# Gated linear attention feeding an ELU feed-forward: one conversion of all weight pairs put on ScalarE, and a new hand-written order for the first ten spans

## The chip, the cores and the metric

The kernel runs on one core of one Trainium2 chip. The metric is the device time of one execution in microseconds (us), the median of several runs. The engines go by the profile's names: PE (matrix products; PEld is its weight load), DVE (VectorE), ACT (ScalarE), POOL (GpSimd) and SP (SyncE, which here issues the DMAs).

## The reference

Four batches of eight heads run a recurrence over 768 steps with a 48x48 state; the result goes, all heads side by side, through a feed-forward layer with an ELU. All inputs are fp32.

```python
for t in range(S):                                   # S = 768, D = 48
    state = alpha[:, :, t, :, None] * state + np.einsum('bhd,bhe->bhde', k[:, :, t], v[:, :, t])
    y[:, :, t] = np.einsum('bhd,bhde->bhe', q[:, :, t], state)
x = y.transpose(0, 2, 1, 3).reshape(B * S, H * D)    # 3072 x 384
h = x @ w_in                                         # 384 x 2048
g = np.where(h > 0, h, np.exp(np.minimum(h, 0)) - 1)
out = g @ w_out                                      # 2048 x 384
```

## The kernel before, in words

**The attention half** works on 24 windows of 128 steps (six per batch), all eight heads at once. For window i the tokens are: `L` (or `LA` and `LB`, its alpha part and its k and q part) loads k, q and alpha, `LV` loads v; `SC` (L214, DVE) scans alpha into running products P; `LN` and `EX` (L223, L228, ACT) make 1/P; `KA`, `KB`, `KC` (L236, L241 on DVE or POOL, L246 on DVE) scale k in three steps; `PC` (L250, ACT) copies P; `SQ` (L263 or L266) scales q; `TP` (L280, PE) transposes k and `KN` (L302, ACT) copies the transpose out of PSUM; `S` (L337 or L321) multiplies k with q, `MK` (L354 or L349, DVE) masks it; `U` (L384 or L366, PE) makes the state's update, `UP`, `UA`, `UB`, `UC` carry the state on; `YL` and `Y` (L445, L492 or L450, PE) give the window's output, with `Y3` (L479, ACT) between them in the first four windows. `XH` (L507, ACT) rounds the output to the upper half of a two-part number; `XL` (L531 on ACT or L533 on DVE) gives the rest; for windows 0 and 1 `XP` (L511, PE) first subtracts the upper part in PSUM.

**The feed-forward half** works on 12 blocks of 256 rows (two windows each) and eight slices j of the 2048 inner columns: `A.b.j` (L656, PE, 18 matmuls) makes h, `RA` and `RB` (L664, L669, ACT) and `RC` (L674, DVE) the ELU, `GH` (L680, ACT) and `GL` (L693, DVE) its two-part form, `O.b.j` (L707, PE, 12 matmuls) the product with w_out.

**The weights** are stored as fp64 and are made into two-part numbers on the chip. `F.f` (L560) loads one of 16 pieces of 768 KB; two pieces make a pair p (f = 0 and 2 are pair 0, f = 1 and 3 pair 1, f = 4 and 6 pair 2, f = 5 and 7 pair 3, and so on). `DA.p` (L577, DVE) shifts the lower words, `DB.p` turns the top byte of each number into the exponent bits by one multiply-add over 1536 bytes per partition, `DC.p` (L592, DVE) joins the two. Then `WH.f` (L620, ACT) rounds the upper part and `WL.f` makes the rest: on POOL or DVE (L640), but for f = 0 and 2 through PE (`WP`, L629 and L511) and ACT (L638). Before the change `DB` stands on DVE (L587) for pairs 0 and 1 and on ACT (L585) for the six others. `LC`, `CA` and `CB` only test the weights' range.

**The order** of everything is written out by hand. A string START lists 546 tokens (with `X.n`, n dummy matmuls on PE, L128), and the kernel issues them one after the other; then a template STEADY is laid out for each later pair of windows and block. Every engine works through its own instructions in the order of issue, so a token that waits holds back all later ones of that engine, and a DMA that waits on SP holds back the later DMAs. PSUM has eight buffers, the k, q and alpha tiles have three slots, the v tiles four. Twelve dummy matmuls stand ahead of START (`X(WARM)`), twelve more in it. START runs to the fifth slice of the fourth block; the rest of the kernel is STEADY.

Of the kernel before, what the change touches and what calls it, by code (L numbers as in the profile page):

```python
# [48 lines left out]


START = """
LA.0 X.2 SC.0 LN.0 LB.0 X.2 EX.0 SQ.0 LA.1 X.1 X.1 X.1 X.1 LV.0 X.1 LB.1 KA.0 SC.1 F.2 LN.1 KB.0 X.1 KC.0 X.1 EX.1 KA.1
PC.0 TP.0 KN.0 F.0 S.0 L.2 KB.1 SQ.1 MK.0 U.0 UA.0 KC.1 TP.1 YL.0 DA.0 S.1 UC.0 DB.0 LV.1 Y3.0 PC.1 L.3 KN.1 SC.2 LN.2
F.3 EX.2 DC.0 KA.2 SQ.2 Y.0 WH.0 U.1 MK.1 F.1 UP.1 UA.1 UC.1 WP.0 F.6 WH.2 YL.1 SC.3 F.4 XH.0 KB.2 LN.3 WP.2 KC.2 EX.3
Y3.1 SQ.3 XP.0 DA.1 WL.0 KA.3 PC.2 WL.2 LV.2 L.4 F.14 X.1 Y.1 DB.1 TP.2 XH.1 LV.3 S.2 KN.2 XP.1 KB.3 F.8 DA.2 XL.0 UB.0
KC.3 XL.1 DC.1 U.2 TP.3 DB.2 WH.1 A.0.0 F.5 UB.2 MK.2 RA.0.0 S.3 WL.1 UC.2 KN.3 UA.2 F.7 YL.2 RB.0.0 DC.2 U.3 F.10
A.0.1 WH.4 SC.4 WL.4 L.5 RC.0.0 LN.4 UA.3 SQ.4 WH.3 A.0.2 Y3.2 GH.0.0 MK.3 DA.3 YL.3 UB.3 EX.4 GL.0.0 WH.6 WL.6 Y.2
KA.4 WL.3 RA.0.1 RB.0.1 Y3.3 RC.0.1 Y.3 UC.3 RA.0.2 DB.3 RB.0.2 RC.0.2 A.0.3 KB.4 UB.1 XH.2 XH.3 GH.0.2 O.0.0 XL.2 XL.3
LV.4 DC.3 F.9 GH.0.1 RA.0.3 GL.0.1 A.1.1 A.1.2 GL.0.2 PC.3 DA.4 RB.0.3 RA.1.1 RC.0.3 GH.0.3 F.12 KC.4 TP.4 LV.7 RB.1.1
DB.4 RA.1.2 O.0.1 WH.7 RC.1.1 RB.1.2 DC.4 SC.5 A.1.0 WH.5 KN.4 L.6 F.11 GL.0.3 WL.5 LC.0 GH.1.1 RC.1.2 U.4 S.4 WH.8  # L60
PC.4 WH.10 DA.5 UB.4 UA.4 WL.7 O.0.2 GL.1.1 A.1.3 RA.1.0 WL.8 RB.1.0 GH.1.2 RC.1.0 RA.1.3 LV.5 L.7 O.0.3 GL.1.2 A.1.4
LN.5 EX.5 DA.6 GH.1.0 SQ.5 RA.1.4 DB.5 MK.4 RB.1.3 GL.1.0 UC.4 DB.6 KA.5 DC.5 RB.1.4 WH.11 WL.10 WH.9 DC.6 RC.1.3
RC.1.4 A.0.4 O.1.0 ZV.6 O.1.1 SC.6 GH.1.3 RA.0.4 RB.0.4 GL.1.3 GH.1.4 A.0.5 RC.0.4 LN.6 WL.11 O.1.2 WL.9 KB.5 WH.14
RA.0.5 GL.1.4 RB.0.5 WH.12 EX.6 RC.0.5 WL.14 O.1.3 O.1.4 GH.0.4 F.15 KC.5 LV.6 GH.0.5 GL.0.4 TP.5 S.5 KN.5 KA.6 PC.5
O.0.4 MK.5 KB.6 CA.0 SC.7 KC.6 WL.12 LN.7 A.0.6 U.5 F.13 GL.0.5 RA.0.6 DA.7 Y.4 UA.5 DB.7 EX.7 RB.0.6 PC.6 DC.7 A.0.7
XH.4 RA.0.7 XL.4 RB.0.7 A.1.7 RC.0.6 WH.13 KA.7 WH.15 WL.13 GH.0.6 O.0.5 RC.0.7 WL.15 GL.0.6 SQ.6 L.8 T.6 GH.0.7 RA.1.7
RB.1.7 GL.0.7 SQ.7 Y.5 A.1.5 XH.5 O.0.6 XL.5 RA.1.5 A.1.6 RC.1.7 GH.1.7 O.0.7 RB.1.5 RA.1.6 XD.4 RC.1.5 KB.7 TM.6 XD.5
RB.1.6 A.2.1 Z.0 RC.1.6 GH.1.5 CB.0 U.6 UA.6 GL.1.5 GH.1.6 KC.7 UB.6 UC.6 RA.2.1 LC.1 SC.8 O.1.5 PC.7 GL.1.6 A.2.0
GL.1.7 S.6 LN.8 RB.2.1 LV.8 S.7 SQ.8 MK.6 T.7 RA.2.0 EX.8 KA.8 O.1.6 RC.2.1 RB.2.0 A.2.3 GH.2.1 RC.2.0 GH.2.0 MK.7 KB.8
TM.7 O.1.7 A.2.2 KC.8 Z.1 GL.2.1 PC.8 GL.2.0 T.8 U.7 UA.7 S.8 MK.8 RA.2.3 CA.1 RA.2.2 Y.6 Y.7 UB.7 A.2.4 O.2.0 O.2.1  # L70
L.9 UC.7 SC.9 XH.6 RB.2.2 RB.2.3 LN.9 L.10 A.2.6 EX.9 RC.2.2 RC.2.3 XH.7 KA.9 GH.2.3 TM.8 LV.9 RA.2.4 XL.6 KB.9 RB.2.4
XL.7 GH.2.2 RC.2.4 SQ.9 CB.1 A.2.5 RA.2.6 KC.9 GH.2.4 GL.2.2 O.2.2 RA.2.5 PC.9 RB.2.6 S.9 GL.2.3 RB.2.5 GL.2.4 U.8 T.9
XD.6 UA.8 UB.8 RC.2.5 UC.8 GH.2.5 XD.7 SC.10 LC.2 TM.9 SQ.10 O.2.3 RC.2.6 A.2.7 LN.10 A.3.1 LV.10 RA.2.7 RB.2.7 GL.2.5
A.3.0 RA.3.1 RC.2.7 CA.2 O.2.4 CB.2 EX.10 MK.9 O.2.5 RB.3.1 LC.3 GH.2.6 GL.2.6 U.9 RA.3.0 O.2.6 RB.3.0 KA.10 RC.3.0
GH.3.0 RC.3.1 A.3.2 UA.9 LV.11 KB.10 UB.9 A.3.3 KC.10 L.12 L.11 UC.9 PC.10 T.10 GH.2.7 RA.3.2 GL.3.0 A.3.4 SC.11 GH.3.1
RB.3.2 GL.2.7 O.3.0 RA.3.4 LN.11 RC.3.2 EX.11 KA.11 GL.3.1 CA.3 SQ.11 O.3.1 RA.3.3 GH.3.2 CB.3 RB.3.3 RB.3.4 GL.3.2
KB.11 TM.10 RC.3.3 RC.3.4 GH.3.3 LC.4 GL.3.3 O.2.7 KC.11 PC.11 T.11 GH.3.4 Z.2 TM.11 O.3.2 GL.3.4
"""


# [10 lines left out]
def gla_elu_ffn(ctx: ExitStack, tc: tile.TileContext, qka, vv, vn, wgt, out):  # L91
    nc = tc.nc
# [487 lines left out]
    @tok  # L580
    def DB(p):

        word, top = parts(p)[1:]
        if p in (2, 3, 4, 5, 6, 7):
            nc.scalar.activation(out=word, in_=top, func=AF.Copy, scale=1.125, bias=-63.4375)  # L585
        else:
            nc.vector.tensor_scalar(out=word, in0=top, scalar1=1.125, scalar2=-63.4375, op0=ALU.mult, op1=ALU.add)  # L587
# [387 lines left out]
```

## Time and profile before

| | us |
|---|---|
| median of 3 runs | 496.06 |
| lowest and highest | 495.91 and 496.23 |
| the profiled execution: its own time | 494.32 |
| its span, first to last instruction | 492.6 |
| PE busy | 485.7 |
| ACT busy | 324.4 |
| DVE busy | 317.2 |
| POOL busy | 132.8 |

The busy time of an engine is the union of its instructions. For PE this says only that matmuls follow each other, since their ends are modelled. Where PE doesn't wait, the order of the other engines costs nothing; a wait of PE is time lost for good. The profiled execution was 1.7 us shorter than the median, and 1.7 us of its own time lie outside its span.

### The profile page before, as it was taken

The numbers are of one execution on the slowest core, as the hardware profiler recorded it, in microseconds if no ns is written. First come the engines' busy times: TensorE is split into PE (matmuls) and PEld (weight loads), VectorE is DVE, ScalarE is ACT, GpSimd is POOL, SyncE is SP. The second block draws the span as 40 slices with busy tenths as digits, with TensorE's granted clock in tenths as the row PEclk, the third lists the DMA queues.
The fourth block names the chain that finished last, engine by engine and source line by source line (L and its number), as shares of the span: only waits on it lengthen the run. The fifth ranks groups of instructions, "written<-read, shape, count | busy, mean of one in ns | idle before, by whom it ended". The sixth has DMA issues, their size and how long they took to land.

```text
span 492.6 us, 13059 instructions
## 1 busy us (share of the span) xinstructions
PE 485.7 (99%) x5348; PEld 469.4 (95%) x5348; DVE 317.2 (64%) x544; ACT 324.4 (66%) x759; POOL 132.8 (27%) x110
## 2 busy tenths in 40 slices
...
GB/s 316 413 415 312 190 2 206 27 110 99 177 53 207 40 150 164 110 104 153 142 81 177 134 78 187 95 110 193 81 126 130 73 133 41 33 38 13 1 35 37
DMA packets 42019, 63.89 MB, mean 130 GB/s; under 512 B 22496, under 2 KB 29408, under 8 KB 41952
## 3 DMA queue, kind: packets, MB, share of 16 engines
...
q8 instruction: 44, 0.72, 0.7%
q10 hardware_dynamic: 288, 0.39, 0.2%
...
HBM read 51.56 MB, written 4.72 MB: 114 GB/s over the span
## 4 chain that ended last, share of the span: by engine, by line
PE 98%; DVE 0%; issue 0%; ACT 0%; DVEq 0%
PE h L656 42%; PE o L707 41%; PE y L450 4%; PE q L321 2%; PE q L366 2%; PE y L445 2%; PE wp L128 2%; PE sc L337 1%; PE tp L280 1%; PE y L492 1%; PE wd L629 1%; PE u L384 0%; PE u L410 0%; PE wd L511 0%; DVE st L354 0%
## 5 line engine op out<-in xcount | busy, mean ns | idle before, releaser
L656 PE MATMUL h<-xt,w 128*128 128x256 f32 x1728 | 216.2, 281 | 0.1
L656 PEld LDWEIGHTS h<-xt,w 128*128 128x128 f32 x1728 | 210.4, 188 | 1.6 <-PE q L366 0.2
L707 PE MATMUL o<-w,gh 128*128 128x384 f32 x768 | 197.1, 338 | 0.0
L707 PEld LDWEIGHTS o<-w,gh 128*128 128x128 f32 x768 | 136.0, 188 | 0.4
L707 PE MATMUL o<-w,gl 128*128 128x384 f32 x384 | 129.3, 337 | 0.0
L674 DVE SCALAR_TENSOR_TENSOR h<-r,h 128x512 f32<-128x512 f32 x96 | 65.6, 692 | 89.2 <-ACT r L669 88.3
L664 ACT ACTIVATE r<-h 128x512 f32<-128x512 f32 x96 | 56.2, 593 | 56.7 <-PE h L656 53.8
L680 ACT CAST gh<-h 128x512 fp32r<-128x512 f32 x96 | 55.4, 583 | 45.4 <-DVE h L674 35.6
L266 POOL TENSOR_TENSOR st<-qka,P 64x512 f32<-64x512 f32 x38 | 46.1, 1214 | 112.4 <-issue 109.7
L707 PEld LDWEIGHTS o<-w,gl 128*128 128x128 f32 x384 | 72.2, 188 | 0.0
L693 DVE TENSOR_TENSOR gl<-h,gh 128x512 fp32r<-128x512 f32 x96 | 63.6, 678 | 10.5 <-ACT gh L680 9.5
L669 ACT ACTIVATE r<-r 128x512 f32<-128x512 f32 x96 | 60.4, 632 | 1.5
L236 POOL TENSOR_TENSOR qka<-qka,R 128x512 f32<-128x512 f32 x19 | 25.8, 1360 | 100.4 <-ACT R L228 85.2
L611 ACT ACTIVATE ck<-ck,lim 128x384 f32<-128x384 f32 x64 | 41.7, 652 | 1.7
L349 DVE TENSOR_TENSOR st<-q,mask 64x256 f32<-64x256 f32 x80 | 33.8, 422 | 6.3 <-PE q L321 2.4
L214 DVE TENSOR_TENSOR_SCAN P<-qka,first 128x516 f32<-128x516 f32 x24 | 35.4, 1474 | 2.1 <-DMA qka<-in_qka_dram 1.8
L241 POOL TENSOR_TENSOR R<-P,R 128x512 f32<-128x512 f32 x20 | 27.9, 1394 | 17.0 <-DVE qka L236 10.1
L223 ACT ACTIVATE R<-P 128x512 f32<-128x512 f32 x24 | 15.1, 627 | 16.0 <-DVE P L214 16.0
L287 DVE STREAM_TRANSPOSE R<-qka 128x512 f32<-128x512 f32 x18 | 19.9, 1105 | 8.8 <-ACT R L250 8.8
L403 DVE TENSOR_TENSOR vs<-vs,q 48x192 f32<-48x192 f32 (+1 forms) x36 | 12.6, 350 | 15.3 <-PE q L366 14.9
L250 ACT ACTIVATE R<-P 128x512 f32<-128x512 f32 x24 | 15.1, 629 | 10.4 <-DVE qka L246 10.4
L450 PE MATMUL y<-st,vs 128*64 128x64 f32 x640 | 21.1, 224 | 0.0
...
## 6 DMA issues: line engine op xcount, KB each, us to landing
...
```

The lines of the kernel that those rows point to most:

```text
L214: nc.vector.tensor_tensor_scan(out=P.rearrange("p n w -> p (n w)"), data0=t[:, 2 * NP * W:], data1=first.rearrange("p n w -> p (n w)"), in ...
L266: eng(SQV, i).tensor_tensor(out=st[r, a], in0=d["q"][r], in1=pw(i)[r], op=ALU.mult)
L349: nc.vector.tensor_tensor(out=d["st"][r, a, :, c * C:(c + 1) * C], in0=d["s4"][a][o], in1=mask[o].unsqueeze(1).broadcast_to([64, NP, C]), ...
L450: nc.tensor.matmul(out[64 * a:64 * a + m], lhsT=lhs(i, c, a)[:, n * D:n * D + m], rhs=d["st"][:, a, n, c * C:(c + 1) * C], start=start, st ...
L611: nc.scalar.activation(out=t[:, :, k], in_=t[:, :, 1], func=AF.Relu, scale=sign, bias=bias, accum_out=chk_w[:, k, f:f + 1])
L656: nc.tensor.matmul(h[:, f, :], lhsT=t[:, wi, ws], rhs=x[:, c, xi, :], start=(f == 0 and k == 0), stop=(k == 8), skip_group_check=True)
L664: nc.scalar.activation(out=r, in_=d["h"], func=AF.Relu, scale=-1.0)
L669: nc.scalar.activation(out=d["r"], in_=d["r"], func=AF.Exp, scale=-1.0)
L674: nc.vector.scalar_tensor_tensor(out=d["h"], in0=d["r"], scalar=-1.0, in1=d["h"], op0=ALU.add, op1=ALU.max)
L680: nc.scalar.copy(out=gh, in_=d["h"])
L693: nc.vector.tensor_tensor(out=gl, in0=d["h"], in1=d["gh"].bitcast(F32), op=ALU.subtract)
L707: nc.tensor.matmul(o[:, 0:DM], lhsT=gt[:, f, ms], rhs=t[:, wi, f * DM:f * DM + DM], start=(j == 0 and f == 0 and k == 0), stop=(j == NJ - ...
```

## The change

It does two things. `DB` goes to ACT for all eight pairs, so that the branch for DVE falls away. And START is written anew: the same 546 tokens, as a set, in another order. STEADY and all other code stay as they are; instructions behind `DB` have line numbers that are smaller by three (L656 is L653 in the changed kernel, L707 is L704).

```diff
 START = """
-LA.0 X.2 SC.0 LN.0 LB.0 X.2 EX.0 SQ.0 LA.1 X.1 X.1 X.1 X.1 LV.0 X.1 LB.1 KA.0 SC.1 F.2 LN.1 KB.0 X.1 KC.0 X.1 EX.1 KA.1
+X.2 LA.0 SC.0 LA.1 X.2 LB.0 LB.1 X.1 F.2 LV.0 X.1 F.0 LN.0 LV.1 X.1 SC.1 EX.0 KA.0 X.1 KB.0 KC.0 X.1 X.1 X.1 X.1 LN.1
...
     def DB(p):
 
         word, top = parts(p)[1:]
-        if p in (2, 3, 4, 5, 6, 7):
-            nc.scalar.activation(out=word, in_=top, func=AF.Copy, scale=1.125, bias=-63.4375)
-        else:
-            nc.vector.tensor_scalar(out=word, in0=top, scalar1=1.125, scalar2=-63.4375, op0=ALU.mult, op1=ALU.add)
+        nc.scalar.activation(out=word, in_=top, func=AF.Copy, scale=1.125, bias=-63.4375)
```

**DVE at the very start**, before the change. The scan L214 makes P of a window; `qka0` is the tile of window 0, `qka1` that of window 1, `st_136` the masked product of window 0.

```order
L214 SCALAR_TENSOR_TENSOR P_128<-qka0_120,first_89 128x516
L236 TENSOR_TENSOR qka0_120<-qka0_120,R_130 128x512
L214 SCALAR_TENSOR_TENSOR P_147<-qka1_121,first_89 128x516
L241 TENSOR_TENSOR R_130<-P_128,R_130 128x512
L246 SCALAR_TENSOR_TENSOR qka0_120<-R_130,qka0_120 128x512
L236 TENSOR_TENSOR qka1_121<-qka1_121,R_151 128x512
L263 TENSOR_TENSOR st_187<-qka1_121,P_147 128x512
L354 TENSOR_TENSOR st_136<-sc_168,mask_85 128x2x4x64
L246 SCALAR_TENSOR_TENSOR qka1_121<-R_151,qka1_121 128x512
L577 TENSOR_SCALAR wm_221<-raw0_149 128x1536
```

The same place in the changed kernel (`st_158` is the masked product of window 0):

```order
L214 SCALAR_TENSOR_TENSOR P_128<-qka0_120,first_89 128x516
L214 SCALAR_TENSOR_TENSOR P_145<-qka1_121,first_89 128x516
L236 TENSOR_TENSOR qka0_120<-qka0_120,R_141 128x512
L241 TENSOR_TENSOR R_141<-P_128,R_141 128x512
L246 SCALAR_TENSOR_TENSOR qka0_120<-R_141,qka0_120 128x512
L236 TENSOR_TENSOR qka1_121<-qka1_121,R_156 128x512
L246 SCALAR_TENSOR_TENSOR qka1_121<-R_156,qka1_121 128x512
L263 TENSOR_TENSOR st_205<-qka1_121,P_145 128x512
L354 TENSOR_TENSOR st_158<-sc_170,mask_85 128x2x4x64
L577 TENSOR_SCALAR wm_232<-raw0_136 128x1536
```

The scan of window 1 no longer stands between the three steps on window 0's k, and window 1's last step (L246) no longer waits behind the mask of window 0 (L354).

**SP, from the second load of window 1 on**, before the change (`raw0` and `raw1` are weight pairs 0 and 1, `qka2` is window 2; the second `qka0` is window 3, in the slot of window 0):

```order
L183 DMA qka1_121<-in_qka_dram 128x1024
L560 DMA raw0_149<-in_wgt_dram 128x6144 x2
L175 DMA qka2_122<-in_qka_dram 128x1540
L191 DMA vs1_106<-in_vv_dram 128x768
L175 DMA qka0_120<-in_qka_dram 128x1540
L560 DMA raw1_253<-in_wgt_dram 128x6144 x2
L560 DMA raw2_315<-in_wgt_dram 128x6144 x2
```

And in the changed kernel:

```order
L183 DMA qka1_121<-in_qka_dram 128x1024
L560 DMA raw0_136<-in_wgt_dram 128x6144
L191 DMA vs0_105<-in_vv_dram 128x768
L560 DMA raw0_136<-in_wgt_dram 128x6144
L191 DMA vs1_106<-in_vv_dram 128x768
L175 DMA qka2_122<-in_qka_dram 128x1540
L560 DMA raw1_244<-in_wgt_dram 128x6144 x2
L175 DMA qka0_120<-in_qka_dram 128x1540
L560 DMA raw2_277<-in_wgt_dram 128x6144
```

Window 3's tile (L175 into `qka0`) was the tenth DMA and is now the twelfth, behind both pieces of weight pair 1; the set of the first twelve is the same.

**ACT from window 3's logarithm to the rest of window 1's output**, before the change (L223 and L228 are `LN.3` and `EX.3`, L638 the casts of `WL.0` and `WL.2`, L507 `XH.1`, L302 `KN.2`, L531 `XL.0` and `XL.1`):

```order
L223 ACTIVATE R_333<-P_327 128x512
L228 ACTIVATE R_333,chk_p_114<-R_333 128x512
L479 COPY y3_343<-y_318 128x128
L638 CAST w0_284<-wd_309 128x384
L638 CAST w0_284<-wd_312 128x384
L250 ACTIVATE R_251,chk_p_114<-P_249 128x512
L638 CAST w0_284<-wd_335 128x384
L638 CAST w0_284<-wd_338 128x384
L507 ACTIVATE xt_330,chk_y_115<-y_318 128x3x128
L302 COPY kn_416<-tp_392 128x512
L531 CAST xt_330<-y_214 128x3x128
L531 CAST xt_330<-y_318 128x3x128
```

And in the changed kernel, where L584 is the multiply-add of pair 1 and L635 are the casts:

```order
L584 ACTIVATE raw1_244<-raw1_244 128x2x768
L223 ACTIVATE R_347<-P_345 128x512
L228 ACTIVATE R_347,chk_p_114<-R_347 128x512
L635 CAST w0_317<-wd_327 128x384
L635 CAST w0_317<-wd_330 128x384
L531 CAST xt_342<-y_237 128x3x128
L507 ACTIVATE xt_342,chk_y_115<-y_308 128x3x128
L302 COPY kn_413<-tp_389 128x512
L635 CAST w0_317<-wd_320 128x384
L635 CAST w0_317<-wd_323 128x384
L531 CAST xt_342<-y_308 128x3x128
```

The conversion of pair 1 now stands ahead of `LN.3`; two casts, `XL.0` and `XH.1` stand between `EX.3` and `KN.2`, and `PC.2` is behind this place.

On PE the twelfth dummy of START goes from behind `XP.0` to the dummies ahead of `TP.0`; `WP.2` and `WP.0` follow each other where `YL.1` stood between them; `S.3` and `TP.3` change places; `TP.4` goes from behind `A.1.2` to the place ahead of `Y.3`, and `U.4` to the place ahead of `O.0.0`. At the end of START, POOL has `SQ.10` behind `SQ.11` instead of far ahead of it.

More of the change, by code (lines that the diff above doesn't have):

```diff
@@ L51 @@
 START = """
-LA.0 X.2 SC.0 LN.0 LB.0 X.2 EX.0 SQ.0 LA.1 X.1 X.1 X.1 X.1 LV.0 X.1 LB.1 KA.0 SC.1 F.2 LN.1 KB.0 X.1 KC.0 X.1 EX.1 KA.1
[L53 to L76, printed above, removed]
@@ L77 @@
-KB.11 TM.10 RC.3.3 RC.3.4 GH.3.3 LC.4 GL.3.3 O.2.7 KC.11 PC.11 T.11 GH.3.4 Z.2 TM.11 O.3.2 GL.3.4
+X.2 LA.0 SC.0 LA.1 X.2 LB.0 LB.1 X.1 F.2 LV.0 X.1 F.0 LN.0 LV.1 X.1 SC.1 EX.0 KA.0 X.1 KB.0 KC.0 X.1 X.1 X.1 X.1 LN.1
+SQ.0 TP.0 EX.1 KN.0 KA.1 KB.1 S.0 KC.1 U.0 SQ.1 MK.0 UA.0 L.2 TP.1 S.1 DA.0 PC.0 KN.1 YL.0 F.3 F.1 PC.1 UC.0 Y3.0 MK.1
+U.1 DB.0 SC.2 LN.2 UP.1 L.3 F.4 LV.2 DC.0 UA.1 Y.0 EX.2 KA.2 YL.1 WH.2 WH.0 WP.2 F.6 WP.0 UC.1 DA.1 F.5 Y3.1 KB.2 F.7
+XH.0 DB.1 SC.3 LN.3 EX.3 SQ.2 KC.2 SQ.3 KA.3 XP.0 Y.1 WL.0 TP.2 XL.0 XH.1 S.2 KN.2 LC.0 KB.3 XP.1 KC.3 DA.2 U.2 LV.3
```

22 lines of the change are left out of this document (added).

## The prediction

> **What bounds the kernel now.** I read the page first, then the waits of PE, then PE's, DVE's and ACT's timelines of the first 45 us. The page's rows of busy time and of the chain that ended last:
>
> ```profile
> PE 485.7 (99%) x5348; PEld 469.4 (95%) x5348; DVE 317.2 (64%) x544; ACT 324.4 (66%) x759; POOL 132.8 (27%) x110
> PE 98%; DVE 0%; issue 0%; ACT 0%; DVEq 0%
> ```
>
> PE is the chain for 98% of the span. The stretches of the span (length, then busy time of PE, PEld, DVE, ACT and POOL, the granted clock, the DMA share, GB/s) say where it isn't busy:
>
> ```profile
> 0.00:5.00 5.00, 2.92 (x7) 1.04 (x8) 2.81 (x10) 1.28 (x1) 2.83 (x13) 1.00 0.60 202
> 5.00:10.00 5.00, 4.60 (x20) 1.96 (x19) 3.40 (x5) 2.99 (x7) 1.19 (x1) 1.00 1.00 381
> 10.00:15.00 5.00, 4.74 (x118) 4.09 (x117) 4.51 (x8) 2.17 (x8) 1.56 (x1) 1.00 1.01 420
> 15.00:20.00 5.00, 5.00 (x89) 4.27 (x89) 4.94 (x7) 3.58 (x8) 1.57 (x1) 1.00 1.02 415
> 20.00:25.00 5.00, 5.00 (x62) 3.42 (x62) 4.91 (x7) 4.26 (x13) 0.00 (x0) 1.00 1.02 412
> 25.00:30.00 5.00, 5.00 (x115) 4.44 (x110) 4.18 (x6) 3.56 (x7) 0.00 (x0) 1.00 1.02 414
> 30.00:35.00 5.00, 4.87 (x102) 4.55 (x102) 5.00 (x5) 3.07 (x6) 3.34 (x1) 1.00 1.02 414
> ```
>
> PE has lost time until 15 us and 0.13 us at 33 us, and nothing else before the tail. DVE is full from 15 to 25 and from 30 to 35 us, the DMA engines from 5 to 35 us. PE's own waits, all of them:
>
> ```profile
> PE wp L128 <- DVE first L122: 2.1, 1, 2.1
> PE tp L280 <- issue: 0.4, 1, 0.4
> PE tp L280 <- DVE qka L246: 0.3, 1, 0.3
> ```
>
> So the same 546 tokens in another order can win about a microsecond here, and lose any amount.
>
> **The change part by part.** PE's timeline at the places that move (start, busy time, the group, the idle time before it):
>
> ```profile
> 2.08 7.22 PE L128 MATMUL wp<-first 128*128 128x512 bf16 x23 [2.08 <-DVE first L122]
> 9.71 0.63 PE L280 MATMUL tp<-ident,qka 128*128 128x128 f32 x4 [0.40 <-issue]
> ...
> 12.88 0.66 PE L280 MATMUL tp<-ident,qka 128*128 128x128 f32 x4 [0.26 <-DVE qka L246]
> ...
> 23.20 0.39 PE L128 MATMUL wp<-first 128*128 128x512 bf16 x1
> 23.52 0.88 PE L492 MATMUL y<-y,sel 128*64 128x128 f32 x12
> ...
> 27.89 0.68 PE L366 MATMUL q<-vs,kn 64*64 64x48 f32 x32
> ...
> 42.04 1.60 PE L445 MATMUL y<-st,vs 48*48 48x64 f32 x48
> ...
> 45.78 0.52 PE L707 MATMUL o<-w,gh 128*128 128x384 f32 x2
> ```
>
> and DVE's:
>
> ```profile
> 6.43 0.73 DVE L236 TENSOR_TENSOR qka<-qka,R 128x512 f32<-128x512 f32 x1 [1.45 <-ACT R L228]
> 7.08 1.22 DVE L214 TENSOR_TENSOR_SCAN P<-qka,first 128x516 f32<-128x516 f32 x1
> 8.22 0.66 DVE L241 TENSOR_TENSOR R<-P,R 128x512 f32<-128x512 f32 x1
> 8.91 0.69 DVE L246 SCALAR_TENSOR_TENSOR qka<-R,qka 128x512 f32<-128x512 f32 x1
> ...
> 26.20 0.96 DVE L577 TENSOR_SCALAR spare<-raw 128x1536 int32<-128x1536 int32 x1 [0.82 <-DMA raw<-in_wgt_dram]
> ```
>
> *TP.0.* It waits for `KC.0`, which ended at 9.60. The scan of window 1 (1.22) goes ahead of `KA.0`, into the 1.45 in which DVE waits for ACT, so `KA.0` at 6.43, `KB.0` and `KC.0` follow each other (0.73, 0.66, 0.69) and end about 8.5 us. But PE is in order and now has 24 dummies ahead of `TP.0` instead of 23: 7.22 us end at 9.30, and one more costs at most 0.27 (16 of them in the 4.3 us from 5 to 9.3). `TP.0` starts at about 9.55: -0.15. Bounds: 0, should `KA.0` be held back by a POOL product until 7.2, and -0.4, all the idle time there.
>
> *TP.1.* Its 0.26 of waiting goes if `KC.1` ends before `U.0` does, which is 2.9 us behind the start of `TP.0` (12.88 - 0.26 - 9.71), at 12.45. `EX.1` follows `EX.0` on ACT and ends near 7.7; `KA.1` starts behind `KC.0` at 8.5 (0.7), `KB.1` on POOL took up to 1.57 (row below), `KC.1` 0.69: about 11.5, a cover of 0.9, if nothing holds them up. -0.26; bounds 0 and -0.4, with the restart.
>
> *The dummy at 23.20* holds PE for 0.32 until `Y.1` starts. At the start it lies in the waiting for `TP.0`, already counted. -0.32; at worst -0.15, if the change of kind in the array costs the rest.
>
> *The 0.13 at 33 us* lies in `U.3`, which now comes behind two `A` groups: -0.13; bounds 0 and -0.3, should the restart behind it have cost as much again.
>
> *The conversions.* The two forms of it and the steps behind it (busy time, mean ns of one, idle time before), then rows of the timelines of ACT and POOL:
>
> ```profile
> L585 ACT ACTIVATE raw<-raw 128x1536 int32<-128x1536 uint8 x6 | 9.8, 1632 | 0.0
> L587 DVE TENSOR_SCALAR raw<-raw 128x1536 int32<-128x1536 uint8 x2 | 1.9, 954 | 0.0
> L592 DVE SCALAR_TENSOR_TENSOR wm<-raw,wm 128x1536 int32<-128x1536 int32 x4 | 7.2, 1796 | 0.7 <-ACT raw L585 0.7
> L620 ACT CAST w<-wm 128x768 fp32r<-128x768 f32 x8 | 6.5, 826 | 0.2 <-DVE wm L592 0.2
> ```
>
> ```profile
> 21.11 0.63 ACT L223 ACTIVATE R<-P 128x512 f32<-128x512 f32 x1 [0.49 <-DVE P L214]
> 21.77 0.63 ACT L228 ACTIVATE R<-R 128x512 f32<-128x512 f32 x1
> 22.31 0.18 ACT L228 ACTIVATION_READ_ACCUMULATOR R<-R 128x1 f32 x1
> ...
> 22.55 0.86 ACT L638 CAST w<-wd 128x384 fp32r<-128x384 f32 x2
> ...
> 25.96 0.49 ACT L507 ACTIVATE xt<-y 128x384 fp32r<-128x384 f32 x1 [1.17 <-PE y L445]
> 26.54 0.59 ACT L302 COPY kn<-tp 128x512 f32<-128x512 f32 x1
> ```
>
> ```profile
> 18.30 1.57 POOL L241 TENSOR_TENSOR R<-P,R 128x512 f32<-128x512 f32 x1 [6.22 <-DVE qka L236]
> 30.83 3.34 POOL L640 TENSOR_TENSOR w<-spare,w 128x768 fp32r<-128x768 f32 x1 [10.96 <-ACT w L620]
> ```
>
> DVE is rid of 2 x 0.95 = 1.9 us, ACT gets 2 x 1.63 = 3.3. From 15 to 35 us ACT was busy for 3.58 + 4.26 + 3.56 + 3.07 = 14.5 of 20 us; it will be for 17.7. That fits, so the conversions as such cost nothing; what they may cost is the lateness of the ACT steps behind them, each of which PE needs. [...]
>
> *The new order around it.* The place where the cover is thinnest: window 3's load was the tenth transfer and is the twelfth. Before, the fourteenth (`F.4`) landed when `DA.2` could start, at about 26.1; two pieces of 768 KB lie between, at 412 GB/s 1.9 us each, so the twelfth lands near 22.3. Then, one behind the other: `SC.3` 1.22, `LN.3` 0.66, `EX.3` with its read 0.72, the two casts of `WL.0` 0.8, `XL.0` 0.49 (as `XH`, the same size), `XH.1` 0.58, `KN.2` 0.59. That is 5.1 us, so `KN.2` ends at 27.4. `U.2` needs it. PE gets to `U.2` at 27.89 - 0.15 - 0.26 - 0.32 = 27.15. A wait of 0.2 is new; bounds 0 and +0.6 (the landing may be some tenths off, since it is worked out from a rate).
>
> *Covered.* Pair 0's conversion follows `Y3.0` on ACT, at about 14.8, and ends at 16.5; `DC.0` 1.80 and two casts of 0.83 make 20.0, and PE asks for the second one at about 20.1, behind `U.1`, `UP.1`, `Y.0`, `YL.1` and the first piece of `WP`. If it is late, PE waits as long; I take nothing. `TP.4` comes earlier, ahead of `Y.3`: PE had 17.9 us from `U.2` to the first `O` (27.89 to 45.78), about 2.4 of them `Y.3` (0.88 and 1.60); so it is at `TP.4` at 27.35 + 15.5 = 42.8. `KC.4` stands on DVE behind `SC.4`, which follows window 3's masks at about 35, `DC.3` 1.80 and five steps of about 0.69 (`KC.0`'s), it is the sixth: 35 + 1.2 + 1.8 + 4.1 = 42.1, a cover of 0.7. Weight pair 3 lands earlier, ahead of its use. STEADY and the tail have the same instructions, and PE waits for nothing there; `SQ.10`, which STEADY reads, is one POOL pair (2.5 us) later than `SQ.11` was, ahead of a first product some 9 us behind it:
>
> ```profile
> 199.85 2.48 POOL L266 TENSOR_TENSOR st<-qka,P 64x512 f32<-64x512 f32 x2
> ```
>
> ```profile
> 211.32 0.66 PE L321 MATMUL q<-st,qka 48*64 48x64 f32 x32
> ```
>
> The sum on the profiled execution: 494.32 - 0.15 - 0.26 - 0.32 - 0.13 + 0.2 = 493.66, that is -0.66, say -0.7. The median of the runs is 1.74 above the profiled one; the same difference taken from it gives 495.4.
>
> **The rivals.** *All covers hold, all gaps close* (faster): TP.0 -0.4, TP.1 -0.4, the dummy -0.32, `U.3` -0.3, nothing new: -1.4, 494.6. Speaks for it that these gaps are all that PE has lost; against it that the dummies themselves fill the first.
>
> *ACT's queue becomes the bound from 20 to 35 us* (slower). It is in order, and `WL`, `XL`, `XH`, `KN` stand behind two conversions and behind window 3's logarithm. PE is held one for one at `U.2` or at `A.0.1` from the point at which `KN.2` ends after 27.15; one conversion on that path is +1.63, so -0.86 + 0.2 + 1.63 = +1.0, 497.0; both are 498.7. A landing of window 3 at 24 us or later does the same. For it: 17.7 of 20 us, and the 0.2 is already the wrong way. Against it: from 10 to 20 us ACT had 4.2 us free, and pair 1's conversion ends (22.0) before window 3 lands (22.3). [...]
>
> *A POOL product holds DVE up ahead of `TP.4`* (no change). This row stood beside the POOL row of 30.83 above:
>
> ```profile
> 32.40 2.86 DVE L214 TENSOR_TENSOR_SCAN P<-qka,first 128x516 f32<-128x516 f32 x1
> ```
>
> The scan took 2.86 instead of 1.23 while POOL's product ran. In the new order `SC.4` stands beside the first such product of pair 2 (about 33 to 36 us), with `DC.3`, `WL.4` and `KC.4` behind it: 1.6 late, of which the cover takes 0.7, so 0.9 is given back: -0.7 + 0.9 = +0.2, 496.3. [...]
>
> *The gaps close, but PE meets the next late input and waits there instead* (no change): 496.1.
>
> **How the numbers follow.** My forecast has 0.40, from 495.0 to 496.0; all gaps close 0.25; ACT the bound 0.18; POOL ahead of `TP.4` 0.12; nothing won 0.05. A measurement of this kernel tells about 0.2%, 1.0 us, from no change (the runs before lie within 0.32 us). Faster by more than that are the second case and a small part of the first (0.06): 0.31. Slower is the third: 0.18. The rest, 0.51, is the same. The range reaches from the second case's 494.6 to one exposed conversion, 497.0; what lies beyond are 0.05 below and about 0.1 above.
>
> **What would show it.** Right: `TP.0` at 9.5 to 9.6 without idle time, `TP.1` right behind `U.0`, no dummy behind `XP.0`, PE at its first `O` group no later than before less 0.7 (without `TP.4` and `U.4`), PE full from 13 us on but for some tenths at `U.2`. Wrong: PE idle in front of L366 or L653 between 25 and 45 us with ACT as the releaser, or in front of `TP.4` with DVE; window 3's scan after 24 us; any gap of PE behind 50 us; or a faster kernel by over 1.0 us with no wait gone that is named here.

## The result, and the profile after

The changed kernel took 498.03 us (median of 20 executions, 495.57 to 502.99); the kernel before, beside it, 496.09 (20 executions, 493.92 to 496.74). The ratio is 1.0063, with a 95% interval of 1.0042 to 1.0084: slower by 0.63%. The forecast was 495.4 with a range to 497.0.

The 20 executions are not one crowd. Five stand at 500.43 to 502.99 with a mean granted clock of 0.983 to 0.988, on average 502.27; the other fifteen average 497.52 with 0.996 to 1.00; before averaged 495.78. So 1.19 of the 2.93 us between the two means (498.71 and 495.78) are the five. The profiled execution is one of them: 502.74 us, span 501.0, clock 0.983. Its page, the row of busy time and the chain by engine:

```profile
PE 491.1 (98%) x5348; PEld 474.2 (95%) x5348; DVE 318.3 (64%) x542; ACT 326.9 (65%) x761; POOL 133.9 (27%) x110
PE 97%; DMA 1%; issue 0%; POOL 0%; SPq 0%; ACT 0%; POOLq 0%
```

PE is busy for 5.4 us more with the same 5348 products, and a DMA, SP and POOL have come onto the chain, where before had only DVE and ACT beside PE. The stretches that the prediction showed of before (length, busy time of PE, PEld, DVE, ACT, POOL, granted clock, DMA share, GB/s):

```profile
5.00:10.00 5.00, 4.24 (x18) 1.67 (x16) 3.14 (x3) 2.59 (x6) 1.68 (x1) 1.00 0.96 349
10.00:15.00 5.00, 3.99 (x70) 3.61 (x71) 3.67 (x7) 0.71 (x2) 1.18 (x1) 0.76 1.04 429
15.00:20.00 5.00, 5.00 (x76) 4.46 (x76) 2.66 (x4) 3.58 (x8) 0.00 (x0) 0.50 1.01 412
20.00:25.00 5.00, 5.00 (x56) 4.14 (x53) 3.72 (x4) 3.11 (x7) 1.18 (x1) 0.50 1.02 417
25.00:30.00 5.00, 5.00 (x41) 3.64 (x37) 3.73 (x5) 3.49 (x8) 0.00 (x0) 0.87 1.01 408
```

From 15 to 30 us PE reads as full; the granted clock, third from the end of the row, is the column that tells. (The clock's record begins only when the clock first comes up: until then, about 5.8 us here, the column reads 1.00 although the dummies start 0.427 us apart instead of 0.216.) Two things stand here: PE lost 1.8 us around 10 us, and then ran at half clock. The beginning of the chain of the first 35 us gives the first:

```profile
1.74 6.06 DMA qka<-in_qka_dram
...
7.95 1.69 POOL st L263
9.64 1.37 issue
11.01 0.63 PE tp L280 x4
```

The DMA is `LB.0`, issued third instead of second, as the new order has `LA.1` ahead of it: it lands at 7.80. The chain goes on with POOL's `SQ.0`, which waits for that landing and in before started at 5.42; the step that ends right ahead of `TP.0` is `KC.0`, at 10.90 in DVE's rows. DVE's rows of the changed kernel go on from there:

```profile
3.72 2.36 DVE L214 TENSOR_TENSOR_SCAN P<-qka,first 128x516 f32<-128x516 f32 x2 [0.83 <-DMA qka<-in_qka_dram]
7.90 0.69 DVE L236 TENSOR_TENSOR qka<-qka,R 128x512 f32<-128x512 f32 x1 [1.82 <-DMA qka<-in_qka_dram]
8.63 1.55 DVE L241 TENSOR_TENSOR R<-P,R 128x512 f32<-128x512 f32 x1
10.21 0.69 DVE L246 SCALAR_TENSOR_TENSOR qka<-R,qka 128x512 f32<-128x512 f32 x1
```

and POOL's, the step beside them:

```profile
7.95 1.68 POOL L263 TENSOR_TENSOR st<-qka,P 128x512 f32<-128x512 f32 x1 [4.32 <-DMA qka<-in_qka_dram]
```

They say that `KA.0` starts 1.47 later than before (7.90, was 6.43). `KB.0` stands beside `SQ.0` and takes 1.55 instead of 0.66, which uses up 0.89 of what the scan's new place wins. `TP.0` starts at 11.01 instead of 9.71: +1.30. The two scans do lie ahead, as forecast.

The second, in half microseconds:

```profile
12.50:13.00 0.50, 0.50 (x15) 0.43 (x12) 0.20 (x1) 0.00 (x0) 0.26 (x1) 0.60 0.99 406
...
26.00:26.50 0.50, 0.50 (x11) 0.43 (x8) 0.50 (x1) 0.02 (x1) 0.00 (x0) 0.75 0.95 393
```

A mean of 0.60 in 12.5 to 13.0 is a fall from 1.00 to 0.50 at 12.6, one of 0.75 a return at 26.25: 13.65 us at half. It doesn't double a group's time:

```profile
12.64 2.12 PE L384 MATMUL u<-vs,kn 128*64 128x48 f32 x32
14.69 1.11 PE L280 MATMUL tp<-ident,qka 128*128 128x128 f32 x4
15.73 1.97 PE L337 MATMUL sc<-st,qka 48*64 48x64 f32 x32
```

The same groups take 1.27, 0.66 and 1.15 at full clock (rows under e1): 1.7 times. So 13.65 us at half lose about 13.65 x (1 - 1/1.7) = 5.6. PE's last products, from the chain of before and of after:

```profile
485.91 2.79 PE o L707 x16
```

and

```profile
485.92 9.12 PE o L704 x52
```

The two chains' products end at 488.70 and 495.04: +6.34, of which 1.30 and 5.6 make 6.9; the rest, about 0.6, is won between. The other 2.1 us of the two spans (492.6 and 501.0) lie behind PE's last product: 3.9 us there before, 6.0 here. Most of it is the transfer of the last output, 1.84 us there and 3.92 here. This is not the change's doing: of the four profiled executions of the changed kernel two have 6.0 and 6.4 us there and two 3.9, and the times of before lie in two groups, near 494.3 and near 496.4, with little between. So a median of twelve can swing by a microsecond, and single steps are judged below by PE's rows. The ratios below leave out an execution that is more than 1.5% longer than the fastest of its kernel, which takes one away from each of e1 (527.79 us, with a clock of 0.85), e6, e7, e12 and e13; but for e1's, these are executions with the half clock, and the medians and the counts of half clocks have them.

### The profile page after: what moved, and what is told of

The parts are those of the page before. It is cut to its first block, busy times and chain, and to the rows that moved or that the text cites. A ratio compares the mean times of both kernels' runs of the same rounds, so it can differ in the third digit from the quotient of the medians.

```text
span 501.0 us, 13055 instructions
## 1 busy us (share of the span) xinstructions
PE 491.1 (98%) x5348; PEld 474.2 (95%) x5348; DVE 318.3 (64%) x542; ACT 326.9 (65%) x761; POOL 133.9 (27%) x110
## 4 chain that ended last, share of the span: by engine, by line
PE 97%; DMA 1%; issue 0%; POOL 0%; SPq 0%; ACT 0%; POOLq 0%
PE h L653 41%; PE o L704 41%; PE y L450 4%; PE q L321 2%; PE q L366 2%; PE y L445 2%; DMA qka<-in_qka_dram 1%; PE sc L337 1%; PE u L384 1%; PE y L492 1%; PE tp L280 1%; PE wd L626 1%; POOL st L263 0%; PE u L410 0%; SPq L179 0%
## 5 line engine op out<-in xcount | busy, mean ns | idle before, releaser
L653 PE MATMUL h<-xt,w 128*128 128x256 f32 x1728 | 214.7, 281 | 0.1
L653 PEld LDWEIGHTS h<-xt,w 128*128 128x128 f32 x1728 | 209.5, 188 | 1.4 <-PE q L366 0.2
L704 PE MATMUL o<-w,gh 128*128 128x384 f32 x768 | 197.9, 339 | 0.0
L704 PEld LDWEIGHTS o<-w,gh 128*128 128x128 f32 x768 | 136.2, 188 | 0.6
L704 PE MATMUL o<-w,gl 128*128 128x384 f32 x384 | 129.6, 338 | 0.0
L266 POOL TENSOR_TENSOR st<-qka,P 64x512 f32<-64x512 f32 x38 | 48.2, 1269 | 99.3 <-issue 80.9
L704 PEld LDWEIGHTS o<-w,gl 128*128 128x128 f32 x384 | 72.1, 188 | 0.2 <-DVE gl L690 0.2
L214 DVE TENSOR_TENSOR_SCAN P<-qka,first 128x516 f32<-128x516 f32 x24 | 33.7, 1407 | 1.1 <-DMA qka<-in_qka_dram 0.8
L403 DVE TENSOR_TENSOR vs<-vs,q 48x192 f32<-48x192 f32 (+1 forms) x36 | 12.6, 349 | 18.4 <-PE q L366 18.0
L529 DVE TENSOR_TENSOR y<-y,y 128x128 fp32r<-128x128 f32 x20 | 5.8, 290 | 26.8 <-ACT xt L507 26.5
L250 ACT ACTIVATE R<-P 128x512 f32<-128x512 f32 x24 | 15.1, 628 | 10.2 <-DVE qka L246 10.2
```

Source lines behind the costliest of these rows:

```text
L214: nc.vector.tensor_tensor_scan(out=P.rearrange("p n w -> p (n w)"), data0=t[:, 2 * NP * W:], data1=first.rearrange("p n w -> p (n w)"), in ...
L266: eng(SQV, i).tensor_tensor(out=st[r, a], in0=d["q"][r], in1=pw(i)[r], op=ALU.mult)
L653: nc.tensor.matmul(h[:, f, :], lhsT=t[:, wi, ws], rhs=x[:, c, xi, :], start=(f == 0 and k == 0), stop=(k == 8), skip_group_check=True)
L704: nc.tensor.matmul(o[:, 0:DM], lhsT=gt[:, f, ms], rhs=t[:, wi, f * DM:f * DM + DM], start=(j == 0 and f == 0 and k == 0), stop=(j == NJ - ...
```

## The experiments

Theory: `LB.0`'s place in the queue makes `TP.0` late, and PE's idle time ahead of `TP.0` lowers its clock in a part of the executions; conversions and the order behind cost nothing of it. The rivals are that the conversions load ACT, that the half clock comes from the load behind 12 us, and that the order behind `TP.0` is worse. "Half" counts the executions with a mean granted clock of 0.993 or less. Of 116 executions of before beside these runs, 2 were such and long (498.62 with 0.989, 501.22 with 0.987); a third has 0.949 on record at 494.93.

```
run  kernel                                     median   ratio to before, 95%     half
     changed kernel                             498.03   1.0063 (1.0042-1.0084)   5 of 20
e1   changed, loads in the old order            495.81   1.0007 (0.9985-1.0029)   0 of 11
e2   changed, 32 dummies                        497.32   1.0030 (1.0009-1.0051)   0 of 12
e3   before, loads in the new order             499.99   1.0071 (1.0040-1.0101)   8 of 12
e4   before, 17 dummies instead of 23           496.27   1.0006 (0.9984-1.0028)   1 of 12
e5   before, all conversions on ACT             496.37   1.0011 (0.9991-1.0031)   2 of 12
e6   e1, TP.4 behind Y.3                        497.20   1.0027 (1.0010-1.0044)   1 of 12
e7   changed, 18 dummies                        496.75   1.0033 (1.0012-1.0053)   1 of 12
e8   changed, SQ.0 on DVE                       496.53   1.0011 (0.9995-1.0026)   0 of 12
e11  before, SC.1 and the dummy moved           494.70   0.9990 (0.9970-1.0011)   1 of 12
e12  changed, beside e13                        497.92   1.0046 (1.0014-1.0077)   3 of 12
e13  e7 again, beside e12                       499.16   1.0046 (1.0010-1.0083)   6 of 12
e15  before, the dummy moved                    496.09   0.9991 (0.9963-1.0019)   1 of 12
```

e1 to e4 ran on one chip, e5 to e8 on a second, e9 to e11 on a third, e12 to e15 on a fourth. Only e13 was timed with the changed kernel, e12, beside it. e9, e10 and e14 are single profiled executions.

**e1**, the loads of the start in the old order:

```diff
-X.2 LA.0 SC.0 LA.1 X.2 LB.0 LB.1 X.1 F.2 LV.0 X.1
+X.2 LA.0 SC.0 LB.0 X.2 LA.1 LV.0 X.1 LB.1 F.2 X.1
```

> The changed kernel with the first loads in the order of before: LB.0 second, LA.1 third, LV.0 ahead of LB.1. Nothing else moves. My theory (the loss is LB.0's place in the queue, and the wait of PE that follows from it): LB.0 lands at 5.3 instead of 7.8, KA.0 follows the scan of window 1 at about 7.1, KC.0 ends at 9.2, TP.0 starts at 9.3 to 9.6 instead of 11.0, the granted clock stays 1.00 from 10 to 30 us, no execution is above 498, and the median is within 0.7 of before (495.4 to 496.5). Rival (the two conversions on ACT, or the order behind 12 us, cost the time): 1.4 to 2 us over before stay, median 497.5 to 498.

PE's rows at the start and at `TP.4`:

```profile
9.67 0.63 PE L280 MATMUL tp<-ident,qka 128*128 128x128 f32 x4 [0.42 <-issue]
10.22 1.15 PE L337 MATMUL sc<-st,qka 48*64 48x64 f32 x32
11.30 1.27 PE L384 MATMUL u<-vs,kn 128*64 128x48 f32 x32
12.50 0.66 PE L280 MATMUL tp<-ident,qka 128*128 128x128 f32 x4
...
43.24 0.63 PE L280 MATMUL tp<-ident,qka 128*128 128x128 f32 x4 [0.54 <-issue]
```

`TP.0` stands at 9.67, `TP.1` has no wait, the clock stays at 1.00, and the ratio is 1.0007 with 0.0022 to both sides: this one edit takes the slowdown away, and conversions and the whole order behind 12 us are still in. But nothing is won either: PE stands 0.54 in front of `TP.4`, which before had not.

**e2**, 8 dummies more:

```diff
-SQ.0 TP.0 EX.1
+SQ.0 X.8 TP.0 EX.1
```

> The changed kernel with 8 more dummies ahead of TP.0, 8 x 0.216 = 1.7 us, just what PE stands idle there. My theory (the half clock from 12 to 27 us comes from that idle time): TP.0 still starts at 11.0, without idle time before it; the direct 1.3 us stay, but the clock stays 1.00 and no execution is above 499; median 496.5 to 498. Rival (the clock falls because of the load that follows, or by chance, not by the idle time): a third of the executions still stand at 500 to 503.

PE's first two rows:

```profile
2.08 9.16 PE L128 MATMUL wp<-first 128*128 128x512 bf16 x32 [2.08 <-DVE first L122]
11.08 0.60 PE L280 MATMUL tp<-ident,qka 128*128 128x128 f32 x4
```

`TP.0` is as late as in the changed kernel, the idle time is gone, and so is the half clock: the highest of twelve is 498.19. Twelve executions alone could miss a share of a quarter by chance; e8, which shortens the idle time in another way, has none in twelve either, and e3, on this chip, has eight. Here `KC.0` ended at 10.49 and the dummies at 11.24, so this filler itself held `TP.0` up by about 0.5.

**e3**, the new order of loads in the kernel before (`LA.0`, `LA.1`, `LB.0`, `LB.1`, `F.2`, `LV.0`):

> The kernel before with the first loads in the order of the changed one (LA.0, LA.1, LB.0, LB.1, F.2, LV.0), nothing else of the change. My theory: LB.0 lands near 7.8, TP.0 starts near 11.0 behind 1.5 to 1.8 us of idle time, the median is 1.3 to 2 us over before, and some executions (a few in twenty, or a third) stand at 500 to 503 with the granted clock at half for some 14 us. Rival (the loss comes from the steps behind TP.0): within 0.5 us of before, no execution above 498.

PE's row of `TP.0`:

```profile
11.80 0.63 PE L280 MATMUL tp<-ident,qka 128*128 128x128 f32 x4 [2.70 <-issue]
```

and the half microseconds in which the clock fell and came back:

```profile
12.50:13.00 0.50, 0.50 (x18) 0.50 (x18) 0.50 (x2) 0.50 (x1) 0.39 (x1) 0.75 0.97 406
...
19.50:20.00 0.50, 0.50 (x11) 0.39 (x9) 0.50 (x1) 0.47 (x2) 0.00 (x0) 0.92 1.09 418
```

Six DMAs in another order make before as slow as the changed kernel and slower: its median is 4.3 us above before's, where 1.3 to 2 were expected, with eight of twelve at half clock. Its `TP.0` is later than expected, since there the scan of window 1 stands between `KA.0` and `KB.0`, and took 2.21 beside `SQ.0`. The clock is at half here from 12.75 to 19.6.

**e4**, `WARM = 12` to `WARM = 6` in before:

> The kernel before with 17 instead of 23 dummies ahead of TP.0. No input is later: TP.0 starts at 9.7 in any case, behind about 1.7 us of idle time instead of 0.4. My theory (idle time of this length can lower the clock): the fastest executions as before, others 6 to 8 us longer with a mean granted clock near 0.983. Rival (only the lateness of an input costs time, and the clock fell for another reason): the median within 0.3 us of before and no execution above 498.

Inconclusive. In the profiled execution the clock of the dummies came up at 7.8 instead of 6.35, the seventeen lasted to 8.73, and the idle time was 1.07, not 1.7. One execution of twelve was at 499.01 with 0.992.

**e5**, in `DB`, the branch for DVE taken out of before:

```diff
-        if p in (2, 3, 4, 5, 6, 7):
...
+        nc.scalar.activation(out=word, in_=top, func=AF.Copy, scale=1.125, bias=-63.4375)
```

> The kernel before with the one edit that all eight conversions stand on ACT; its order unchanged. My theory (the conversions cost nothing): the median within 0.3 us of before, TP.0 at 9.7, PE's last product ends at 488.7 to 489.3 (before 488.69). Rival (ACT becomes the bound from 15 to 35 us): one or two conversions appear as waits of PE in front of Y.1, WP or A groups, PE ends 1.6 us or more later, the median 1.4 to 3 us above before.

PE's waits behind the first dummy:

```profile
PE tp L280 <- issue: 1.6, 1, 1.6
PE y L492 <- ACT w L635: 0.2, 1, 0.2
```

No wait for a conversion; the 0.2 behind `WL` stands in e3 and e4 as well, with the old conversions. So they cost nothing that shows. The median is 0.85 above before's, past the 0.3 expected, but the ratio tells no difference (1.0011 with 0.0020 to both sides). That the profiled execution is long (498.21) has another cause: `LA.1`, third in the old order, landed at 7.5 (5.9 in before), `TP.0` started at 10.15 behind 1.57 idle, and the clock was at half from 11.7 to 18.5. So the kernel before can meet this as well (2 of its 116 executions were long with a low clock); the change meets it more often.

**e6**, e1 with `TP.4` and `KN.4` behind `Y.3`:

```diff
-A.0.2 TP.4 XH.2 UC.3 WH.7 RA.0.3 XL.2 WL.3 F.14 KN.4 RB.0.3 GL.0.1 Y.3 WH.5
+A.0.2 XH.2 UC.3 WH.7 RA.0.3 XL.2 WL.3 F.14 RB.0.3 GL.0.1 Y.3 TP.4 KN.4 WH.5
```

> The kernel of the first experiment (loads in the old order) with TP.4 and KN.4 behind Y.3 again, as they stood before the change. There PE waited 0.54 us in front of TP.4, for KC.4, which ended at 43.14. My theory (the forecast gain of 0.7 was made by 30 us and given back in front of TP.4): no wait in front of TP.4 and none at Y.3, PE's last product ends 0.4 to 0.6 earlier than in the first experiment (at 488.6 to 488.8), the median about 0.5 lower. Rival (Y.3's own input is as late): the wait moves to Y.3 and PE's end stays at 489.2.

PE's waits behind the first dummy:

```profile
PE q L366 <- DVE h L671: 0.7, 1, 0.7
```

A miss: the wait moved to `U.4` (L366), the products behind `TP.4` (0.67), and PE ended at 489.56. `LA.1` landed at 6.9, so `TP.0` was 0.61 later than in e1 and PE's end only 0.35 (489.21 there); how much of the difference is the edit's can't be told. It looks as if PE waited from 35 to 47 us for DVE's and ACT's whole row of steps and not for one token; no run tries that by itself.

**e7**, `WARM = 12` to `WARM = 6` in the changed kernel:

> The changed kernel with 18 instead of 24 dummies ahead of TP.0, whose inputs stay as they are: TP.0 at 11.0 in any case, behind 2.3 to 3.3 us of idle time instead of 1.8. [...] Rival (the half clock has nothing to do with the idle time): the same spread as the changed kernel, median near 498, a quarter of the executions at 500 or more.

A miss for the theory, which has more half clocks with more idle time, and "`TP.0` at 11.0 in any case" is wrong as well. In the profiled execution `LB.0` landed at 6.18, `TP.0` started at 9.61 behind 0.98 idle, the clock stayed. One of twelve was at half. This chip's share had no counterpart of the changed kernel beside it; e12 and e13 repeat it with one.

**e8**, `SQ.0` on DVE behind `KC.0`:

```diff
-WLV, KAV, KBV, SQV = (0, 4), (0, 1, 2, 3, 10), (0, 3, 5, 6), (1, 2, 3, 5)
+WLV, KAV, KBV, SQV = (0, 4), (0, 1, 2, 3, 10), (0, 3, 5, 6), (0, 1, 2, 3, 5)
```

> The changed kernel with SQ.0 on DVE behind KC.0 instead of on POOL; the loads stay in the new order. In the changed kernel KB.0 took 1.55 us beside POOL's SQ.0, and 0.66 before. My theory: KB.0 takes 0.7 again, KC.0 ends at 10.0 instead of 10.9, TP.0 starts at 10.1 behind 0.9 of idle time, no execution is above 499.5, the median is 0.8 to 1 us below the changed kernel's (497 to 497.3). Rival (KB.0 was slow for another reason, such as the transfers that land beside it): KB.0 stays at 1.5 us and TP.0 at 11 or later, since SQ.0 now stands on DVE as well.

DVE's rows of `KA.0`, `KB.0` and `KC.0`:

```profile
7.95 0.69 DVE L236 TENSOR_TENSOR qka<-qka,R 128x512 f32<-128x512 f32 x1 [1.95 <-DMA qka<-in_qka_dram]
8.68 0.69 DVE L241 TENSOR_TENSOR R<-P,R 128x512 f32<-128x512 f32 x1
9.40 0.69 DVE L246 SCALAR_TENSOR_TENSOR qka<-R,qka 128x512 f32<-128x512 f32 x1
```

`LB.0` landed as late as in the changed kernel, and `KB.0` takes 0.69: `TP.0` at 10.20, no half clock, and the highest of twelve is 498.09. The 0.89 belongs to POOL's product beside it.

**e9 and e10**, the changed kernel unaltered, two more profiled executions:

> The changed kernel once more, unaltered, for another profiled execution. So far LB.0, as the third transfer, landed between 6.2 and 7.9 in the five executions profiled with the new order of loads, and as the second between 5.1 and 5.3. [...]

> [...] A quarter of its executions should show the half clock.

e9 (502.82 us): `LB.0` landed at 7.32. PE's row of `TP.0`, and the half microseconds in which the clock fell and came back:

```profile
10.52 0.63 PE L280 MATMUL tp<-ident,qka 128*128 128x128 f32 x4 [1.66 <-issue]
```

then

```profile
11.50:12.00 0.50, 0.50 (x22) 0.50 (x18) 0.00 (x0) 0.27 (x1) 0.50 (x1) 0.83 0.97 399
25.00:25.50 0.50, 0.50 (x16) 0.50 (x13) 0.50 (x2) 0.00 (x0) 0.00 (x0) 0.51 1.04 430
```

e10 (494.63 us): `LB.0` landed at 5.50, earlier than the 6.2 to 7.9 so far, and `KA.0`, beside `SQ.0`, took 1.20, where DVE's step beside it took 1.55 to 1.66 in the changed kernel, e2, e7 and e9. PE's rows of `TP.0`, `TP.1`, an A group and `TP.4`:

```profile
9.58 0.60 PE L280 MATMUL tp<-ident,qka 128*128 128x128 f32 x4
12.39 0.66 PE L280 MATMUL tp<-ident,qka 128*128 128x128 f32 x4
...
40.48 2.15 PE L653 MATMUL h<-xt,w 128*128 128x256 f32 x16 [0.31 <-DVE w L637]
43.19 0.63 PE L280 MATMUL tp<-ident,qka 128*128 128x128 f32 x4 [0.56 <-issue]
```

The same program, with PE's last product at 494.74 and at 488.92: 5.8 us apart, behind a landing that differs by 1.8 us.

**e11**, before with `SC.1` ahead of `KA.0` and its twelfth dummy ahead of `TP.0`:

> The kernel before with two pieces of the change and no other: SC.1 ahead of KA.0, and the dummy that stood in front of Y.1 at 23.2 us moved ahead of TP.0. Loads, conversions and all else as before. My theory: TP.0 at 9.6 to 9.7 where LA.1 lands by 6 us (one scan's stretch later where it lands at 7 or later), TP.1 without its wait of 0.26, no dummy at 23.2, PE 0.3 to 0.6 earlier at 170 us, if no later input holds it; PE's last product ends at 488.1 to 488.4, the median up to 0.5 below before. Rival (as in the first experiment, PE only meets a later input and waits there): a new wait of 0.3 to 0.6 between 25 and 45 us, PE's end at 488.7, the median as before.

Not told apart: 0.9990 with the 1 inside. In the profiled execution `LA.1` landed at 7.73 and held `SC.1`, and now `KA.0` behind it: `TP.0` at 11.13. PE ended at 489.39, 0.7 later than before with a `TP.0` that is 1.42 later, so about 0.7 was won behind it. Against the expectation `TP.1` still waits 0.26 there, as before.

**e12 to e14**, the changed kernel and e7's kernel on one chip:

> The changed kernel, timed on the same chip as the next run. My theory: one to four of twelve executions at 500 or more, with a mean granted clock of 0.979 to 0.992; the others 495 to 498.6.

> The changed kernel with 18 dummies, beside the changed kernel on the same chip. [...]

> The kernel with 18 dummies, one more profiled execution. [...]

The half clock came in 3 of 12 with 24 dummies and in 6 of 12 with 18: the way that more idle time would have it, but twelve each is too little to tell. In e14 `LB.0` landed at 7.21 and `TP.0` came at 10.40, yet the clock stayed at 1.00, against the theory. PE's row, then the stretches:

```profile
10.40 0.63 PE L280 MATMUL tp<-ident,qka 128*128 128x128 f32 x4 [1.98 <-issue]
```

with

```profile
10.00:15.00 5.00, 4.59 (x111) 4.12 (x113) 3.71 (x7) 2.16 (x6) 1.18 (x1) 1.00 1.04 429
15.00:20.00 5.00, 5.00 (x113) 4.36 (x110) 4.58 (x6) 4.56 (x10) 0.26 (x1) 1.00 1.01 410
```

1.98 us idle and no fall, where 1.57 in e5 were followed by one. What differs is where the idle time lies. The trace has the moment when the clock first comes up: the dummies start 0.427 apart before it and 0.2155 after, and the one interval between the two gives the instant. Counted from there, the eight executions with the most idle time ahead of `TP.0` (all times in us; "behind" is the distance from the instant at which the clock came up):

```
run      clock up   idle ahead of TP.0   TP.0   behind   fall    behind   back
e5       4.87       1.57                 10.15  5.28     11.7    6.83     18.5
e9       5.01       1.66                 10.52  5.51     11.83   6.82     25.5
changed  5.79       1.76                 11.01  5.22     12.6    6.81     26.25
e3       5.93       2.70                 11.80  5.87     12.75   6.82     19.6
e14      6.76       1.98                 10.40  3.64     none
e13      6.25       1.85                 10.03  3.78     none
e4       7.81       1.07                  9.81  2.00     none
e7       7.14       0.98                  9.61  2.47     none
```

All four falls stand 6.81 to 6.83 us behind the rise, though the end of the idle time lies 0.95 to 1.59 ahead of them, and the clock came back about twice or three times as far behind the rise (18.5 - 4.87 = 13.63; 25.5 - 5.01 = 20.49; 26.25 - 5.79 = 20.46; 19.6 - 5.93 = 13.67). It fell where the idle time was 1.57 us or more and ended 5.22 to 5.87 us behind the rise, and did not where 1.85 and 1.98 us ended 3.78 and 3.64 behind it.

The ends of the executions say more. These are two stretches of e9, the first with PE's last products, of 384 columns, then two of before:

```profile
493.11:496.53 3.42, 1.63 (x10) 1.30 (x8) 0.00 (x0) 0.96 (x2) 0.00 (x0) 1.00 0.30 104
496.53:499.94 3.41, 0.00 (x0) 0.00 (x0) 0.00 (x0) 0.00 (x0) 0.00 (x0) 1.00 0.06 18
```

```profile
487.62:491.03 3.41, 1.07 (x7) 0.75 (x5) 0.00 (x0) 0.96 (x2) 0.00 (x0) 1.00 0.33 120
491.03:492.60 1.57, 0.00 (x0) 0.00 (x0) 0.00 (x0) 0.00 (x0) 0.00 (x0) 0.50 0.02 5
```

In e9 PE's last product ended at 494.74, and the clock stood at 1.00 for the 5.2 us from there to 499.94; in before it fell at 491.03, 2.3 us behind the last product, and in the changed kernel at 497.29, 2.3 us as well. So the length of the idle time alone does not decide. Whether it is the kind of work beside it or the place of the idle time behind the clock's rise is not told apart, and no run tries either by itself.

**e15**, only the dummy of e11:

```diff
-KC.0 X.1 EX.1
...
-L.4 F.14 X.1 Y.1
+KC.0 X.1 X.1 EX.1
...
+L.4 F.14 Y.1
```

> The kernel before with one piece of the change: the dummy in front of Y.1 moved ahead of TP.0. My theory: nothing at 23.2 us, 0.3 us earlier from there on, PE's last product ends 0.2 to 0.3 earlier than 488.7 plus what TP.0 is later than 9.71; the median 0.3 below before, within the noise. Rival (a later input takes it): U.3 or an A group waits 0.3 longer, PE's end unchanged.

PE's row of `TP.0`, and those of `XP.0` and `Y.1`, between which the dummy stood:

```profile
9.54 0.63 PE L280 MATMUL tp<-ident,qka 128*128 128x128 f32 x4 [0.59 <-issue]
...
22.87 0.34 PE L511 MATMUL y<-xt,minus 128*128 128x384 f32 x1
23.14 0.88 PE L492 MATMUL y<-y,sel 128*64 128x128 f32 x12
```

Nothing stands between the two rows any more, and PE's last product ends at 488.40, 0.29 earlier than before. Of that 0.17 is `TP.0`, which is earlier for its input; behind it only 0.12 is left of the dummy's 0.32, and PE waits 0.21 in front of an A group where before had no wait, as the rival has it. A gain of that size is below what twelve executions can tell (0.9991 with 0.0028 to both sides). No version was found that beats before by more than its uncertainty.

## Why the prediction was wrong, point by point

**TP.0 is the step that failed.** The prediction took `KA.0` "at 6.43", from before's row, where ACT's exponential was last. That holds only if `LB.0` has landed; I followed window 3's load, but not the exchange of `LA.1` and `LB.0` at the head of SP's list, which stands ahead of the part that the section on the change shows. No rival had this path either: the one slower case was ACT's, and it did not come. In the trace of before the third transfer landed at 5.91 against the second's 5.28, which looks like 0.6 us of cost; over all profiled executions the third lands at 5.5 to 7.9 (17, whichever load it is), the second of the old order, `LB.0`, at 5.05 to 5.4 (7). One profiled execution could not show that. Forecast 9.55; measured 11.01, 10.52, 9.58 and 10.80 in four executions of the changed kernel. The bound that I gave, `KA.0` held by POOL until 7.2, had a POOL product in it and not the landing behind which both start.

**The clock was no term of the sum.** The rows of before had 1.00 in every stretch, and I took it as given. Here 1.76 us of idle time ahead of `TP.0` was followed by half clock, which cost about 5.6 us more; in e5 1.57 us was. What decides on the falls, beyond their 6.81 to 6.83 us behind the rise in four executions, is not shown.

**The conversions**: right. No PE wait names them in e5, e1 or e10; the rival in which ACT becomes the bound did not come.

**TP.1, the dummy, U.3**: right, where `TP.0` is on time: in e10 `TP.1` starts at 12.39 without a wait (12.88 before), no dummy stands at 23 us, the waits have no row of `U.3`. In e12 and e14, two of the executions with a late `LB.0`, `U.3` waits for a load that the prediction doesn't have, window 3's v (`LV.3`): it landed at 35.4 and 34.5, against 31.8 in before, and cost 0.77 and 0.33. PE's row of it in e12:

```profile
35.50 0.68 PE L366 MATMUL q<-vs,kn 64*64 64x48 f32 x32 [0.77 <-DMA vs<-in_vv_dram]
```

`U.2`'s forecast wait of 0.2 did not come either (PE full from 20 to 30 us in e10).

**The sum behind it** failed by 0.9 even so. e10, with `TP.0` as forecast, has PE's last product at 488.92 instead of 488.70 - 0.66 = 488.04. What was won by 35 us went again in front of an A group (0.31, and its 36 products took 2.64 + 2.15 = 4.79 in two pieces, where e6 has 4.59 in one) and `TP.4` (0.56). The prediction gave `TP.4` a cover of 0.7 (`KC.4` to end at 42.1, PE there at 42.8); measured, `KC.4` ended at 43.1, as DVE's rows of e10 show:

```profile
35.57 1.23 DVE L214 TENSOR_TENSOR_SCAN P<-qka,first 128x516 f32<-128x516 f32 x1 [1.09 <-DMA qka<-in_qka_dram]
...
38.37 2.05 DVE L637 TENSOR_TENSOR w<-spare,w 128x768 fp32r<-128x768 f32 x1
...
42.41 0.68 DVE L246 SCALAR_TENSOR_TENSOR qka<-R,qka 128x512 f32<-128x512 f32 x1
```

The scan of window 4 waits 1.09 for its load, which the new order issues behind more weight pieces, and `WL`'s product takes 2.05 beside POOL (0.93 before): the third rival's mechanism, in part. From about 170 to 438 us, where all run the steady template (between the first `Y` products next to these times), the eleven executions with the new START take 267.10 to 267.35 us and the six with the old one 266.79 to 266.86: 0.3 more, seen in part as 0.3 to 0.4 more busy time of the 384-column products in e1 and e10; six of the eleven also show a wait of 0.14 in front of an A group at 222 to 227 us. The prediction put this at nothing ("the same instructions"). The conversions are not it, since e5, one of the six, has all of them on ACT; its cause stays open.

**The range** missed for both reasons: the fifteen executions without the half clock average 497.52, so the late landing with what follows it is past 497.0 by itself, and the five with it add 1.19 to the mean.

Open: why the third transfer's landing varies by over 2 us; why the clock returns after 6.8 us in e3 and e5 and after 13.65 in e9 and the changed kernel; how the 1.74 us by which the fifteen other executions lie above before divide. The one of that kind with a profile and a late `LB.0`, e12, has PE's last product at 491.14, 2.44 later than before: 1.09 of it is `TP.0`, and 0.77, 0.31 and 0.56 are the waits at `U.3`, an A group and `TP.4`, against what was won.
